# Linear attention and a softplus-erf block on one core: one more of nine blocks multiplies g by w_out with seven quarter products

## The chip, the cores and the metric

The kernel runs on one core of a Trainium2 chip. The core has five engines that run side by side, each with its own queue of instructions: TensorE (PE, matrix products into the eight banks of PSUM), VectorE (DVE), ScalarE (ACT), GpSimd (POOL) and SyncE (SP, which here issues nearly all transfers). They wait for each other through semaphores. The metric is the device time of one execution in microseconds (us), as the median of several runs. Lower is better.

## The reference

Attention with a feature map, for 8 batches of 8 heads, 576 tokens and head dimension 64; then a block of two products on the 4608 tokens of 512 values:

```python
def phi(x):
    proj = np.einsum('bhsd,df->bhsf', x, w_phi)
    proj = proj - np.max(np.abs(proj), axis=-1, keepdims=True)
    return np.concatenate([np.exp(proj), np.exp(-proj)], axis=-1)
q_p, k_p = (phi(q), phi(k))
kv = np.einsum('bhsf,bhsd->bhfd', k_p, v)
z = np.sum(k_p, axis=2)
num = np.einsum('bhsf,bhfd->bhsd', q_p, kv)
den = np.einsum('bhsf,bhf->bhs', q_p, z)[..., None] + 1e-06
x = num / den                        # heads side by side: 4608 x 512
...
h = x @ w_in                         # 512 x 2048
sp = np.maximum(h, 0.0) + np.log1p(np.exp(-np.abs(h)))
g = h * erf(sp)
out = g @ w_out                      # 2048 x 512
```

## The kernel before

**Blocks, units, steps.** The tokens of the second part are cut into nine blocks of 512 (`NS = 9`). Blocks 0 to 7 are the first 512 tokens of each batch; block 8 collects the last 64 of all batches. The hidden dimension d_ff is cut into four units of 512 (`NU = 4`). So there are 36 steps, and each step makes h of one unit of one block and then takes g of an earlier unit times w_out. The attention of batch b + 1 is spread over the steps of block b.

**Three terms for one product.** Values and weights are kept as a high and a low fp16 part, and each product is the sum of three matmuls: high by high, high by low, low by high. `mm` (L579, issued at L584) issues each of them as two matmuls on 64 columns of the array each, one per half of the output partitions, that run side by side.

**Seven quarter products.** h is made for all nine blocks after Strassen and Winograd: x and w_in are cut into quarters, seven sums and differences of the quarters of each are formed (x by `split` and `combine`, L942 and L976, with nine tiles `x` in all; w_in by `split_weights`), and seven products of half the size, added up in `add` and `snap`, take the place of eight. `product` (L1107) issues one of them.

**g times w_out has two forms.** The constant `OW` names the first block that uses the second form; it is 4, so blocks 0 to 3 use the first and blocks 4 to 8 the second.

- The first form, `o_piece` (L1358): matmuls of 512 columns, four token tiles by sixteen slices of d_ff by three terms. In `erf_gate` g is made by one multiplication of h and erf (L1207), a conversion to fp16 on ScalarE (L1210) and a subtraction for the low part (L1215), on tiles of 1024 columns. The sums come in two rounds of half of d_ff each: the first round's are evicted (L1379 or L1381) and stored to DRAM (tile `part`, L1383), the second's fetched from there and added (L1387, L1388).
- The second form, `o_chunk` (L1283): seven quarter products of 256 columns for each unit pair and round, fourteen pieces of twelve terms in each round, each evicted or added to tiles in SBUF (L1335, L1338; the very last in two halves at L1326). `g_forms` (L1220) makes the quarters and their sums from g (L1202 the multiplication, L1239 the sums, `split_g` the high part on ScalarE through L602 and the low part on DVE at L1233), seven forms for each unit in eighteen tiles `gf`. The forms of w_out are made once by `t_forms` (L1253) on GpSimd (L1264, L1269, L1279) and stored to DRAM (tile `td`); each round fetches eight tiles of them (L1294).

**Where `t_forms` stands.** It has eight parts, two rounds of four. One part is called in each step from step `TW_FROM` = 10 on. The pieces of a round of g times w_out stand two steps behind the step of the same number, so with block 4 the second form is first read in step 18.

**What sets the order.** Nothing is issued where the code calls it. Each operation is recorded by `Plan.op` with an engine, a cost, its buffers and a priority, its position in the nominal course of PE's work plus an offset. `Plan.run` (L290) then plays the five engines forward, and gives each engine, whenever it is free, the ready operation of the lowest priority; an operation is ready when its inputs and a free tile for its output are there. Tiles of one kind are handed out in the order of the calls. Operations of DVE and GpSimd that are marked `port` are kept from overlapping. The order so found is fixed in the program, for SP's queue of transfers as well.

**The table of shifts.** `SHIFT` changes single priorities: when the planned time of PE passes a key, the operations with the listed numbers get the listed nanoseconds added to their base priority. The numbers are those of the calls (`o.seq`).

```python
while shifts and free["PE"] >= shifts[0][0]:
    for seq, by in shifts.pop(0)[1].items():
        self.ops[seq].prio = self.ops[seq].base + by
```

**Attention.** Groups of four tiles go through `project` (L797), `front` (the maximum at L740, the subtraction at L756), two exponentials on ScalarE, a transposition (`t_piece`, later `turn` with a DMA, L842 to L845), `kv_piece` and `n_piece` (matmuls at L594, evictions at L874, L910 and L918). Nearly all of the evictions are on DVE.

Of the kernel before, what the change touches and what calls it, by code (L numbers as in the profile page):

```python
# [95 lines left out]
SLACK = 1000.0  # L96
WARM = 7
HOLE = 600.0
OW = 4
GF = 18  # L100
OC = 8
TW_FROM = 10
TW_STEP = 1
TW_POOL = 1
OW_ODD = (1, 1, 1, 1, 1, 1, 1)
# [25 lines left out]
OSB_ACT = 0, 2  # L131
OC_ACT = 9, 9
SHIFT = {
# [38 lines left out]
}  # L172
PRINT = None
EXP_LN = "natural_log_exp_and_others"
# [2 lines left out]
def early(name, step):  # L177

    return EARLY.get(name, globals()[name]) if step < NE else globals()[name]
# [22 lines left out]
class Plan:  # L202
# [27 lines left out]
    def op(self, eng, cost, fn, r=(), w=(), done=None, off=0.0, mode=COLS, land=0.0, port=False, need=None, give=None):  # L230
        o = Op()
        o.eng, o.cost, o.fn, o.mode, o.land, o.port = eng, cost, fn, mode, land, port
        o.slack = self.slack
        o.need, o.give = need, give
        o.stay = self.stay
        o.after = None
        o.late = self.late
        o.step = self.step
        o.done = cost + 120.0 if done is None else done
        o.seq = len(self.ops)  # L240
        o.base = o.prio = self.pos + off
        o.succ, o.unmet, o.ready, o.start = [], 0, 0.0, None
        o.bufs = []
        o.open = o.bufs
        deps = {}

        def touch(item, write):
            b, key = item if isinstance(item, tuple) else (item, None)
            if b not in o.bufs:
                o.bufs.append(b)  # L250
                b.left += 1
            known = write
            for k, (ws, rs) in b.state.items():
                if k is None or key is None or k == key:
                    known = True
                    for d in ws:
                        deps[d] = True
                    if write:
                        for d in rs:
                            deps[d] = True  # L260
            assert known, "read before it is written"
            if write:
                if key is None:
                    b.state.clear()
                b.state[key] = ([o], [])
            else:
                b.state.setdefault(key, ([], []))[1].append(o)

        for item in r:
            touch(item, False)  # L270
        for item in w:
            touch(item, True)
        deps.pop(o, None)
        for d in deps:
            d.succ.append(o)
        o.unmet = len(deps)
        self.ops.append(o)
        return o
# [188 lines left out]
def favor_attention_moe(ctx: ExitStack, tc: tile.TileContext, qk, vp, wphi, w_in, w_out, out):  # L467
# [716 lines left out]
    def erf_gate(n, after):  # L1184
# [12 lines left out]
        op(ACT, 2230, last, w=pair[1:], done=1070, need="erf", give="exp", off=GATE_AT[2])  # L1197
        if n[0] >= OW:
            h0, h1 = hs.pop((n, 0)), hs.pop((n, 1))
# [195 lines left out]
    todo = [(s, 2 * r + i) for s, r in rounds for i in range(2)]  # L1395
    half_rounds = [(s, r, t if s < OW else 7 * t) for s, r in rounds for t in range(2)]
    SIZE = lambda x: range(4) if x[0] < OW else range(x[2], x[2] + 7)
    steps = [[todo[i] if i < len(todo) else None, []] for i in range(len(todo))]
    for i, o in enumerate(half_rounds):
        later = TAIL[1] if i >= len(todo) - TAIL[0] else OW_LAG if o[0] >= OW else 0  # L1400
        steps[min(i + 2 + later, len(todo) - 1)][1].append(o)
# [3 lines left out]
    def moe_step(h, o):  # L1405
        prods = h_unit(h) if h else []
        last = h == todo[-1]
        mix = (0,) * 7 if last else (OW_ODD if o[0][2] else OW_EVEN) if o and o[0][0] >= OW else early("O_ODD", plan.step) if o and o[0][2] == 1 else early("O_EVEN", plan.step)
        left = [(x, i) for x in o for i in SIZE(x)]
        o_part = lambda x, i: o_chunk(x, i) if x[0] >= OW else o_piece(x, i)  # L1410
        for c, f in enumerate(prods):
# [52 lines left out]
    for n, (h, o) in enumerate(steps):  # L1464
        plan.step = n
        if forms and n >= TW_FROM and (n - TW_FROM) % TW_STEP == 0:
            t_forms(*forms.pop(0))
# [90 lines left out]
```

## Time and profile before

| what | value |
|---|---|
| time, median of three runs | 935.15 us (934.76 to 935.24) |
| the profiled execution | 934.75 us |
| its span from first to last instruction | 932.9 us |
| granted TensorE clock | 0.999 |
| matmuls | 17226, of which 1536 of 512 columns |
| transfers | 185.75 MB |

A page of the profile shows one execution. "Busy" is the time in which an engine has an instruction at work; register, branch, semaphore and DMA-issuing instructions are not counted. Matmuls overlap in the array and their ends are modelled, so the busy time of PE is no sum of its instructions' lengths, and the rate has to be read from counts and times of stretches. PEld is the loading of weights into the array, which overlaps the matmuls. In groups of instructions, each row has the line of the code, the engine, the operation, output <- inputs, the count, then busy time and mean length of one, then the idle time of the engine ahead of them and what ended it. Rows of stages have for each engine the busy time and the number of instructions, then the granted clock, the busy share of the DMA engines and GB/s.

### The profile page before, as it was taken

What the parts mean: (1) busy time and instruction counts of PE and PEld (TensorE: products, weight loads), DVE (VectorE), ACT (ScalarE), POOL (GpSimd) and SP (SyncE); (2) the same over time, 40 slices, a digit from 0 to 9 for tenths busy, and PEclk for the clock granted to TensorE, in tenths of its full rate; (3) what the DMA queues carried; (4) which work ended last, traced back from release to release, by engine and by line L of the source; (5) the groups of instructions that cost most, each with busy time, mean ns of one, the idle gap of its engine ahead of it and who ended that gap; (6) DMA issues with size and microseconds to landing.
All of it is one profiled execution on the core that took longest, in us unless ns stands there. A gap on an engine that the chain in (4) does not pass through costs nothing.

```text
span 932.9 us, 38966 instructions
## 1 busy us (share of the span) xinstructions
PE 920.2 (99%) x17226; PEld 813.9 (87%) x17226; DVE 803.7 (86%) x1462; ACT 736.3 (79%) x1164; POOL 192.9 (21%) x201
## 2 busy tenths in 40 slices
PE   8999999999999999999999999999999999999998
PEld 7788877878787878778787899999999999999997
DVE  6999999999768786888877999999999878777875
ACT  7898989797978777877777778968777788779792
POOL 0352120010455657110211020100201241010000
PEclk9999999999999999999999999999999999999999
DMA  9489999999865969467867768686857675782502
GB/s 336 131 232 300 288 231 327 316 316 298 216 163 178 215 166 245 121 168 186 198 149 183 236 142 204 171 222 192 199 119 185 209 197 168 241 192 81 164 32 47
DMA packets 199273, 185.75 MB, mean 199 GB/s; under 512 B 127168, under 2 KB 137536, under 8 KB 199104
## 3 DMA queue, kind: packets, MB, share of 16 engines
q1 hardware_dynamic: 198800, 183.06, 72.2%
q8 instruction: 135, 2.21, 1.0%
q14 instruction: 34, 0.28, 0.1%
q10 hardware_dynamic: 304, 0.20, 0.1%
HBM read 125.80 MB, written 28.05 MB: 165 GB/s over the span
## 4 chain that ended last, share of the span: by engine, by line
PE 84%; DVE 11%; ACT 2%; issue 2%; DMA 1%; SPq 0%; POOL 0%; DVEq 0%; ACTq 0%
PE bank L584 64%; PE bank L594 12%; PE bank L797 5%; DVE m L740 1%; ACT big L602 1%; DVE half L1233 1%; PE bank L828 1%; PE bank L1501 1%; DVE big L1207 1%; DVE half L756 1%; DVE big L1239 1%; DVE big L1132 1%; DVE big L918 1%; DMA half<-td 1%; DVE big L1202 0%
## 5 line engine op out<-in xcount | busy, mean ns | idle before, releaser
L584 PEld LDWEIGHTS <-half 128*64 128x64 f16 x9432 | 512.4, 110 | 74.0 <-issue 2.0
L584 PE MATMUL bank<-half,half 128*64 128x256 f16 x6456 | 381.3, 273 | 0.0
L584 PE MATMUL bank<-woh,half 128*64 128x512 f16 (+1 forms) x1984 | 252.7, 328 | 1.3 <-DVE big L756 0.8
L584 PE MATMUL bank<-wol,half 128*64 128x512 f16 (+1 forms) x992 | 166.5, 328 | 0.0
L602 ACT ACTIVATE big<-big 128x512 f32<-128x512 f32 x200 | 124.1, 629 | 46.8 <-DVE big L756 23.5
L602 ACT ACTIVATE big<-bank 128x512 f32<-128x512 f32 x190 | 111.2, 611 | 42.9 <-PE bank L584 40.2
L952 POOL TENSOR_TENSOR half<-big,half 128x512 f16<-128x512 f32 x54 | 63.4, 1176 | 365.4 <-DVE half L949 135.7
L602 ACT ACTIVATE half<-big 128x512 f16<-128x512 f32 x140 | 81.2, 622 | 57.7 <-DVE big L1239 51.9
L740 DVE TENSOR_REDUCE m<-bank 128x4 f32<-128x512 f32 x144 | 92.7, 683 | 12.6 <-PE bank L797 12.3
L1132 DVE SCALAR_TENSOR_TENSOR big<-bank,big 128x512 f32<-128x512 f32 x108 | 73.8, 685 | 29.8 <-PE bank L584 18.8
L1233 DVE TENSOR_TENSOR half<-big,half 128x512 f16<-128x512 f32 x140 | 92.5, 694 | 2.7 <-ACT half L602 1.7
L584 PE MATMUL bank<-half,wi 128*64 128x256 f16 x1512 | 93.4, 273 | 0.4 <-issue 0.4
L584 PEld LDWEIGHTS <-wi 128*64 128x64 f16 x1512 | 81.1, 110 | 4.3 <-issue 1.4
L594 PEld LDWEIGHTS bank<-v,big 128*64 128x64 f32 x2016 | 76.5, 138 | 6.8 <-issue 0.7
L594 PE MATMUL bank<-v,big 128*64 128x65 f32 (+1 forms) x2016 | 81.9, 228 | 0.4 <-ACT big L602 0.4
L594 PE MATMUL bank<-kv,big 128*64 128x65 f32 x2304 | 81.7, 222 | 0.6 <-DVE big L918 0.5
L594 PEld LDWEIGHTS bank<-kv,big 128*64 128x64 f32 x2304 | 76.3, 138 | 3.8 <-DVE big L918 0.9
L1179 ACT ACTIVATE big<-big 128x1024 f32<-128x1024 f32 x72 | 72.7, 1050 | 1.1 <-DVE half L640 0.7
L1202 DVE TENSOR_TENSOR big<-big,big 128x1024 f32<-128x1024 f32 x40 | 49.5, 1262 | 19.3 <-ACT big L1196 19.3
L756 DVE TENSOR_TENSOR half<-bank,m 128x512 f32<-128x512 f32 x72 | 49.0, 683 | 0.1
L1207 DVE TENSOR_TENSOR big<-big,big 128x1024 f32<-128x1024 f32 x32 | 39.8, 1267 | 9.6 <-ACT big L1196 9.4
L1196 ACT ACT_TABLE_LOAD x36 | 46.2, 1283 | 0.6
(73 smaller groups left out, 1167.2 us busy)
## 6 DMA issues: line engine op xcount, KB each, us to landing
half<-wd SPq DMA_DIRECT2D x189, 256.0 KB, 4.4
half<-td SPq DMA_DIRECT2D x80, 256.0 KB, 4.6
ld<-in_qk_dram SPq DMA_DIRECT2D x31, 576.0 KB, 4.9
v<-in_vp_dram SPq DMA_DIRECT2D x28, 325.0 KB, 4.8
big<-in_moe_w_in_dram SPq DMA_DIRECT2D x32, 256.0 KB, 5.8
big<-in_moe_w_out_dram SPq DMA_DIRECT2D x16, 512.0 KB, 6.9
out_dram<-half SPq DMA_DIRECT2D x32, 256.0 KB, 2.8
wd<-half SPq DMA_DIRECT2D x21, 256.0 KB, 4.7
```

Source lines behind the costliest of these rows:

```text
L584: nc.tensor.matmul(o[half], a[:, half], b, start=start, stop=stop, **kw)
L594: nc.tensor.matmul(o[half], a[:, half], b, start=first and c == 0, stop=last and c == 1)
L602: nc.scalar.activation(out_(), in_(), func, **k)
L740: op(DVE, 600, lambda: nc.vector.tensor_reduce(m.t, ps(), axis=AX.X, op=ALU.max, apply_absolute_value=True), r=[b], w=[m])
L756: op(DVE, 600, lambda: nc.vector.tensor_tensor(to(), ps(), m.t.unsqueeze(2).to_broadcast([P, GT, NF]), op=ALU.subtract), r=[b, m], w=[key])
L797: nc.tensor.matmul(both[nm].t[:, t * P : (t + 1) * P], x()[rows], w.t[rows, :], start=i == 0, stop=i == len(terms) - 1)
L952: op(POOL if pool else DVE, 1160 if pool else 600, lambda: eng.tensor_tensor(tv(1), view(), tv(0), op=ALU.subtract), r=[*reads, (t, 0)], w ...
L1132: op(DVE, 640, lambda: nc.vector.scalar_tensor_tensor(h.t[:, c * 512 : c * 512 + 512], b.t, HSCALE, h.t[:, c * 512 : c * 512 + 512], op0=A ...
L1179: fn = lambda: nc.scalar.activation(L.t, h.t, AF.Softplus, scale=1.0 / SG)
L1202: op(DVE, 1140, lambda h=h, L=L: nc.vector.tensor_tensor(h.t, h.t, L.t, op=ALU.mult), r=[L, h], w=[h], port=True, off=GATE_OFF[0] * (v + 1))
L1207: op(DVE, 1140, lambda h=h, L=L: nc.vector.tensor_tensor(h.t, h.t, L.t, op=ALU.mult), r=[L, h], w=[h], port=True, off=GATE_OFF[0] * (v + 1))
L1233: op(POOL if pool else DVE, 1160 if pool else 600, lambda: eng.tensor_tensor(hv(1), src(), hv(0), op=ALU.subtract), r=[key, (g, 0)], w=[(g ...
```

## The change

Block 3 takes the second form: `OW` goes from 4 to 3, so six blocks of nine use the seven quarter products. `t_forms` is called from step 6 on instead of step 10. And the table `SHIFT` is a new one throughout, with about twice as many entries; since the numbers of the calls are others from step 6 on, its entries can't be matched with the old ones. No function changes.

```diff
-OW = 4
+OW = 3
 GF = 18
 OC = 8
-TW_FROM = 10
+TW_FROM = 6
 TW_STEP = 1
 TW_POOL = 1
...
 SHIFT = {
-    0.0: {22: 3000, 30: 1000, 33: 1000, 59: -2000, 61: 6000, 68: 10822, 96: 4905, 101: 3905, 107: -2000,
...
-    705000.0: {7172: -3000, 7186: 6000},
+    0.0: {13: -8000, 44: 906, 61: 6000, 80: 1000, 92: 906, 116: -300, 123: -6000, 147: 1000, 182: -4000,
...
+    705000.0: {7044: 1, 7046: 2, 7366: 6000, 7482: 6233, 7493: 6000, 7553: -4000, 7702: -6000, 7704: -3000,
+        7947: -3617, 7973: -2000},
 }
```

With `OW = 3` the nominal positions change with it: a piece of the first form counts 10400 ns and one of the second 9160 (`pe_time`), by which the attention is paced against the steps.

88 rows, old and new, of the table SHIFT are left out of this document.

## The prediction

> **What bounds the kernel now.** I read the page's head first, then the busy time by stage, then what TensorE (PE) waits for, then the chain that ended last.
>
> ```profile
> span 932.9 us, 38966 instructions
> PE 920.2 (99%) x17226; PEld 813.9 (87%) x17226; DVE 803.7 (86%) x1462; ACT 736.3 (79%) x1164; POOL 192.9 (21%) x201
> ```
> ```profile
> core 0: us, PE busy (x) PEld busy (x) DVE busy (x) ACT busy (x) POOL busy (x), PEclk, DMA share, GB/s
> 0.00:150.00 150.00, 143.63 (x2655) 121.07 (x2657) 135.63 (x311) 129.18 (x328) 38.84 (x44) 1.00 0.88 259
> 150.00:400.00 250.00, 250.00 (x4304) 197.35 (x4301) 212.10 (x371) 203.55 (x295) 88.31 (x102) 1.00 0.83 228
> 400.00:550.00 150.00, 149.89 (x2832) 123.58 (x2830) 125.85 (x227) 111.08 (x150) 21.82 (x19) 1.00 0.72 184
> 550.00:700.00 150.00, 148.36 (x3156) 144.72 (x3152) 146.97 (x268) 119.44 (x171) 17.94 (x16) 1.00 0.73 180
> 700.00:729.40 29.40, 29.40 (x668) 28.93 (x664) 28.76 (x57) 23.52 (x33) 3.38 (x3) 1.00 0.67 182
> 729.40:765.00 35.60, 35.60 (x658) 35.60 (x654) 30.86 (x50) 26.39 (x36) 10.80 (x9) 1.00 0.82 224
> ```
> ```profile
> PE bank L797 <- DVE big L756: 0.8, 1, 0.8
> PE bank L584 <- DVE big L756: 0.8, 1, 0.8
> PE bank L584 <- DVE half L1326: 0.5, 1, 0.5
> ```
>
> The stages show PE full from 150 us on. Its only idle time between 150 and 765 us is 0.11 us in 400 to 550 and 1.64 us in 550 to 700. The third fence is the complete list of waits of PE from 150 us to the end: two of 0.8 us (these are the 1.64) and the one before the very last product. The granted clock is 1.00. So the span is the work that PE is given, plus some 6.4 us that it stands idle in the first 150 us. But look at VectorE (DVE): in 550 to 700 us it is busy 146.97 of 150, that is 98%, and this is the one stretch of the middle where PE waits, both times for DVE. The kernel has one bound and a second one right behind it.
>
> **Where the change lands.** Block 3 is the block that changes its form.
>
> ```profile
> L1207 DVE TENSOR_TENSOR big<-big,big x8: 1214/1222/1715, 403.1 to 483.8; 128x1024 f32<-128x1024 f32 x8
> L1388 DVE SCALAR_TENSOR_TENSOR half<-bank,half x4: 682/685/689, 497.5 to 528.6; 128x512 f32<-128x512 f32 x4
> L740 DVE TENSOR_REDUCE m<-bank x144: 652/682/698, 6.2 to 713.1; 128x4 f32<-128x512 f32 x144
> L1264 POOL TENSOR_TENSOR half<-woh,wol x16: 1147/1156/1628, 226.3 to 369.4; 128x512 f32<-128x512 f16 x16
> ```
>
> L1207 is h times erf in the plain form, so its last eight (two to a unit, four units) are block 3: its gates run from 403 to 484 us. The last four L1388 are its second round, ended by 529 us. The attention, which shares DVE with all this, goes on until after 713 us (L740). The change therefore extends to about 400 us the stretch in which seven products and attention run together, which until now begins near 510.
>
> **PE.** The plain form streams 512 columns per matmul, the seven products stream 256. I need the issue pitch of both.
>
> ```profile
> 225.39 36.67 PE bank L584 x482
> 729.43 198.28 PE bank L584 x3628
> ```
> ```profile
> L584 PE MATMUL bank<-woh,half 128*64 128x512 f16 x128 | 20.2, 380 | 0.0
> L584 PE MATMUL bank<-half,half 128*64 128x256 f16 x288 | 17.6, 273 | 0.0
> L584 PE MATMUL bank<-wol,half 128*64 128x512 f16 x64 | 12.3, 379 | 0.0
> ...
> L584 PE MATMUL bank<-half,wi 128*64 128x256 f16 x2 | 0.3, 272 | 0.0
> ```
>
> These are two pieces of the chain, and the groups by form inside the first of them. The second piece holds 256-column matmuls alone: 198.28 / 3628 = 0.05465 us each. The first has 128 + 64 = 192 of 512 columns and 288 + 2 = 290 of 256. The latter take 290 x 0.05465 = 15.85 us, so the wide ones take (36.67 - 15.85) / 192 = 0.1084 us. (The "mean ns" of 273 and 380 are lengths with the pipeline in them and can't be summed.) By the code, block 3 now issues 4 token tiles x 16 slices of d_ff x 3 terms x 2 halves = 384 wide matmuls: 41.6 us. After, 2 rounds x 14 pieces x 12 x 2 = 672 narrow ones: 36.7 us. **PE gains 4.9 us.**
>
> One rule speaks against reading PE so. The Trainium skill, "Perfetto Trace Analysis", section "Identifying the Most-Contended Engine", says that a PE's matmul busy share is a poor measure and that the busy share of weight loads should be judged instead. Here that share goes from 79% (197.35 of 250) to 100% (35.60 of 35.60) where seven products run, and the change adds 288 loads; what that would make of the sum is the last rival. The two pitches decide against it here: each matmul of either width has one load of 64 columns, and the wide one takes 1.98 times as long.
>
> **DVE and ScalarE.**
>
> ```profile
> L1207 DVE TENSOR_TENSOR big<-big,big 128x1024 f32<-128x1024 f32 x32 | 39.8, 1267 | 9.6 <-ACT big L1196 9.4
> L1215 DVE TENSOR_TENSOR half<-big,half 128x1024 f16<-128x1024 f32 x32 | 40.3, 1272 | 1.8 <-ACT half L1210 1.6
> L1388 DVE SCALAR_TENSOR_TENSOR half<-bank,half 128x512 f32<-128x512 f32 x16 | 11.0, 687 | 4.4 <-PE bank L584 4.4
> L1202 DVE TENSOR_TENSOR big<-big,big 128x1024 f32<-128x1024 f32 x40 | 49.5, 1262 | 19.3 <-ACT big L1196 19.3
> L1233 DVE TENSOR_TENSOR half<-big,half 128x512 f16<-128x512 f32 x140 | 92.5, 694 | 2.7 <-ACT half L602 1.7
> L1239 DVE TENSOR_TENSOR big<-big 128x512 f32<-128x512 f32 x40 | 28.3, 708 | 0.1
> L1239 DVE TENSOR_TENSOR big<-big,big 128x512 f32<-128x512 f32 x40 | 27.4, 686 | 0.2
> L1338 DVE SCALAR_TENSOR_TENSOR half<-bank,half 128x512 f32<-128x512 f32 x49 | 33.4, 684 | 9.6 <-PE bank L584 9.5
> L602 ACT ACTIVATE half<-big 128x512 f16<-128x512 f32 x140 | 81.2, 622 | 57.7 <-DVE big L1239 51.9
> L1210 ACT CAST half<-big 128x1024 f16<-128x1024 f32 x32 | 33.1, 1044 | 0.1
> ```
>
> The plain rows cover four blocks and the others five. Block 3 loses 39.8/4 + 40.3/4 + 8 evictions of 0.687 = 25.5 us of DVE. It gains 49.5/5 (gate) + 92.5/5 (low parts) + (28.3 + 27.4)/5 (sums) + 14 evictions of 33.4/49 = 0.68 each, which is 9.9 + 18.5 + 11.1 + 9.5 = 49.0 us. **DVE has 23.5 us more to do, to save PE 4.9.** ScalarE has 81.2/5 - 33.1/4 = 8.0 us more, on 111.08 of 150: I cost that at nothing, since it stays near 82% of a stretch shortened to 145.1; without that cover it would cost up to the 8.0.
>
> What hides the 23.5? In 400 to 550 us DVE would have 125.85 + 23.5 = 149.4 us to do. At the density of the next stretch (98%) that takes 152.4 us, and PE's share of the stretch is now 145.1: **7.3 us too much** if all of it must be done there. Over 400 to 765 us, up to the end of attention and a little past it, it is 125.85 + 146.97 + 28.76 + 30.86 + 23.5 = 355.9, or 363.2 us at 98%, against 365 - 4.9 = 360.1: 3.1 too much. Before 400 us there is room: 212.10 of 250 is 33 us short of 98%. So some of the attention of the blocks that follow has to be done before 400, or some of the work of 400 to 550 after 700. The order can do part of that, as the planner issues whatever is ready. But x has nine tiles and a block keeps seven until its last unit, so attention can't run more than two of the seven forms ahead.
>
> How much PE then waits is not shown for this stretch. Its ends are 0 (the room before 400 takes enough) and 7.3 us (none moves). The nearest row is the stretch that already has both kinds of work: 1.64 us idle in 150. I take that rate for the newly filled 150 + 65 us: 215/150 x 1.64 - 0.11 = **2.2 us**.
>
> **The other parts.** The forms of w_out (POOL, from 226 us on, 16 x L1264 and what follows) are called four steps earlier. Their first reader moves four steps too, and POOL is busy 88.31 of 250 there, so nothing; if they came due among the other transfers before 250 us, a late one would be at most the 0.8 us that the longest wait above shows. DMA:
>
> ```profile
> half<-td SPq DMA_DIRECT2D x80, 256.0 KB, 4.6
> part<-half SPq DMA_DIRECT2D x16, 256.0 KB, 4.7
> half<-part SPq DMA_DIRECT2D x16, 256.0 KB, 4.0
> ```
>
> Sixteen fetches from td come (80 for five blocks), four stores to part and four loads from it go: 2 MB more, with DMA at 0.72 in that stretch. Each fetch waits on SP's queue for an eviction of the same round, and behind it queue the transposes of attention and of x. Again I take nothing, since such fetches stand among 550 to 700 already and are in its 1.64; a late one in each round would be 2 x 0.8 = 1.6 us. The new order may also change the 6.4 us that PE idles before 150. No row says which way: I take 0, and for the ends a third of it, 2.1, up or down.
>
> **The sum.** The profiled execution took 934.75 us, 1.85 around its span; the median of the runs is 935.15, 0.4 above it. 934.75 - 4.9 + 2.2 = 932.05, and 932.4 on the scale of the median.
>
> **The rivals.**
> 1. DVE's room elsewhere takes it all, and the order also regains idle time of the first 150 us: stall 0 to -2.1, 930.2 down to 928.1. For it: 33 us of room before 400. Against: the nine x tiles, and both waits of PE in the middle are for DVE.
> 2. DVE gives back most of it: a stall of 3.1 (the sum over 400 to 765) to 6.7, that is 933.3 to 936.9. For it: that sum. Against: room before 400.
> 3. **Slower: DVE becomes the bound of 400 to 550.** Nothing moves out, PE waits the 7.3 us: 934.75 - 4.9 + 7.3 + 0.4 = 937.6, and 939.2 with a late fetch in both rounds. It decides once less than about half a microsecond of the 7.3 can leave the stretch. For it: the x tiles tie the attention to its block. Against: in 550 to 700 all of this already runs with PE idle 1%.
> 4. Loads, not columns, set PE's pace: 288 more at 0.05465 us is +15.7, so 950.9. By the page named above this would be so; the pitches deny it.
>
> **How the numbers follow.** About 0.2% (1.9 us) is what a measurement of this kernel can tell from no change: faster is below 933.3, slower above 937.0. Forecast (930.2 to 933.3) 0.47, rival 1 0.11, rival 2 0.24, rival 3 0.17, rival 4 0.01. So faster 0.58, same 0.24, slower 0.18. The range goes from 929.0 to 938.5: it leaves out the lower part of rival 1 (0.05), the upper part of rival 3 (0.10) and rival 4.
>
> **What would show it.** PE: 672 narrow matmuls more, 384 wide ones fewer, both pitches unchanged. DVE: 803.7 becomes about 827, and 400 to 550 us goes from 125.85 to over 140. ScalarE about 744. The long stretch of L584 at the end keeps its length and starts some 2 to 5 us earlier. PE's idle time between 400 and 765 rises from 1.75 to about 4 us, its waits named DVE; near 0 is rival 1, above 7 rival 3. The prediction is wrong in its base if PE's idle time in the first 150 us changes by more than 2.1 us, or if the waits name POOL, SP or DMA.

## The result: 0.3% slower

The changed kernel takes 937.53 us as the median of 8 runs (936.78 to 940.33), the kernel before, on the same chip, 934.76 (934.05 to 935.24). The ratio is 1.0033 with a 95% interval of 1.0022 to 1.0044: slower by 2 to 4 us, 2.8 by the medians. The profiled execution of the changed kernel took 936.78 us, the lowest of its eight, with a span of 935.0; before it was 934.75 and 932.9. All lines from 173 on are 17 higher in the changed kernel, since the new table is longer: L601 is the L584 of before, L1250 its L1233, L1219 its L1202.

First the head of the page and then the stages of the changed kernel, with the columns of before: length, PE, weight loads, DVE, ACT and POOL busy (instructions), granted clock, DMA share, GB/s.

```profile
span 935.0 us, 39702 instructions
PE 921.1 (99%) x17546; PEld 831.5 (89%) x17546; DVE 822.6 (88%) x1504; ACT 742.4 (79%) x1184; POOL 191.5 (20%) x201
```
```profile
0.00:150.00 150.00, 145.56 (x2706) 122.85 (x2708) 137.10 (x315) 130.24 (x328) 38.37 (x44) 1.00 0.90 264
150.00:400.00 250.00, 249.78 (x4280) 196.43 (x4278) 211.90 (x368) 201.31 (x294) 87.45 (x102) 1.00 0.83 225
400.00:550.00 150.00, 146.84 (x3070) 139.24 (x3068) 143.01 (x264) 118.29 (x171) 19.20 (x17) 0.99 0.74 192
550.00:700.00 150.00, 148.59 (x3148) 144.74 (x3146) 143.79 (x264) 118.03 (x167) 20.30 (x17) 1.00 0.79 192
700.00:729.40 29.40, 29.15 (x673) 28.01 (x670) 29.37 (x56) 22.21 (x33) 3.55 (x3) 1.00 0.56 137
```

The place to look at first is 400 to 550 us. DVE goes from 125.85 to 143.01 there, and PE's idle time from 0.11 to 3.16. That is most of what the stages show. The longest waits of PE from 150 us to the end name ScalarE and DVE:

```profile
PE bank L611 <- ACT big L619: 2.3, 3, 1.3
PE bank L601 <- DVE big L773: 1.2, 1, 1.2
PE bank L814 <- DVE big L935: 0.7, 2, 0.4
```

The work itself behaved as worked out: the groups by form, and the last long piece of the chain, say so.

```profile
L601 PE MATMUL bank<-woh,half 128*64 128x512 f16 x768 | 121.9, 380 | 0.1
L601 PE MATMUL bank<-wol,half 128*64 128x512 f16 x384 | 73.6, 379 | 0.0
```
```profile
795.55 134.51 PE bank L601 x2454
```

768 + 384 = 1152 wide matmuls are left of 1536, that is 384 fewer, and the narrow ones still come every 134.51 / 2454 = 0.0548 us. So PE has 4.9 us less to do and the span is 2.1 us longer: for 7.0 us more than before PE does no useful work in these two executions (7.7 by the medians). Two places hold most of what can be seen of that. At the first, PE multiplies for nothing: the planner fills a gap of its plan with matmuls on a constant tile (`hot`), to keep the array's clock up. These are the groups on that tile between 150 and 200 us, of the kernel before and of the changed one:

```profile
L1501 PE MATMUL bank<-hot 128*64 128x512 f16 x8 | 1.0, 380 | 0.0
```
```profile
L1518 PE MATMUL bank<-hot 128*64 128x512 f16 x30 | 3.4, 379 | 0.0
```

PE counts as busy all the same, so a gap that was planned doesn't show as idle time; it has to be looked for under this tile's name. The 30 stand at 177.67 us. No operation of the sixth block has run by then, and the first one of `t_forms` (L1281, the L1264 of before) starts only at 201.6 us, so this gap goes with the new order and not with DVE's load in 400 to 550. In the first 150 us there are more of them too, 10.3 us against 9.2:

```profile
L1501 PE MATMUL bank<-hot 128*64 128x512 f16 x62 | 9.2, 437 | 1.5 <-DVE hot L1507 1.5
```
```profile
L1518 PE MATMUL bank<-hot 128*64 128x512 f16 x72 | 10.3, 429 | 1.5 <-DVE hot L1524 1.5
```

The second place is near 535 us. From the timeline of the changed kernel (start, length, engine, line, output <- inputs, count, and in brackets the idle time before it and what ended it):

```profile
525.66 0.60 ACT L619 ACTIVATE big<-bank 128x512 f32<-128x512 f32 x1 [2.61 <-PE bank L601]
...
528.75 2.00 ACT L1196 ACTIVATE big<-big 128x1024 f32<-128x1024 f32 x2
...
530.13 0.68 DVE L773 TENSOR_TENSOR big<-bank,m 128x512 f32<-128x512 f32 x1
...
534.09 1.28 ACT L1211 ACT_TABLE_LOAD   x1
535.38 0.63 ACT L619 ACTIVATE big<-big 128x512 f32<-128x512 f32 x1
...
536.07 0.34 PE L611 MATMUL bank<-v,big 128*64 128x65 f32 x4 [1.30 <-ACT big L619]
...
537.11 1.13 PE L611 MATMUL bank<-v,big 128*64 128x65 f32 x16 [0.70 <-ACT big L619]
```
```profile
535.00:540.00 5.00, 3.23 (x54) 3.06 (x56) 4.49 (x8) 4.93 (x10) 0.00 (x0) 0.70 0.92 219
```

DVE subtracts the maximum of a group of attention (L773) at 530.13, and the exponentials of that group (L619) could follow at 530.8. But ScalarE's queue holds a whole gate ahead of them, softplus from 528.75 and erf with its table loads until 535.4. PE has nothing else left and waits 1.30 and 0.70 us; its clock falls to 0.70 in these 5 us, which costs up to 1.5 us more. DVE is not out of it, though: in the 25 us ahead of this gap it is busy without a pause, and its subtraction comes only after the gate has started on ScalarE. In the kernel before it was nearly as full in the same 25 us, 24.19, and PE didn't wait.

```profile
510.00:535.00 25.00, 24.77 (x530) 23.42 (x524) 25.00 (x44) 17.06 (x24) 0.00 (x0) 1.00 0.81 209
```

The sum of what can be seen: 2.4 us of matmuls on `hot` near 178 us (3.4 - 1.0), 3.05 of idle time in 400 to 550, 0.2 each in 150 to 400 and 700 to 729, less 0.8 in the first 150 us (1.9 less idle time, since 143.63 busy became 145.56, but 1.1 more on `hot`), and less 0.2 each in 550 to 700 and behind 729. That is 4.7, with the clock 6.2 at most. Where the rest of the 7.0 lies is not shown; gaps that the modelled lengths of the matmuls cover would not appear in these rows.

### The profile page after: what moved, and what is told of

It is laid out like the page before. It is cut to its first block, busy times and chain, and to the rows that moved or that the text cites. A ratio compares the mean times of both kernels' runs of the same rounds, so it can differ in the third digit from the quotient of the medians.

```text
span 935.0 us, 39702 instructions
## 1 busy us (share of the span) xinstructions
PE 921.1 (99%) x17546; PEld 831.5 (89%) x17546; DVE 822.6 (88%) x1504; ACT 742.4 (79%) x1184; POOL 191.5 (20%) x201
## 5 line engine op out<-in xcount | busy, mean ns | idle before, releaser
L601 PEld LDWEIGHTS <-half 128*64 128x64 f16 x9720 | 527.5, 110 | 59.0 <-issue 4.3
L601 PE MATMUL bank<-half,half 128*64 128x256 f16 x6840 | 403.9, 273 | 1.5 <-DVE big L773 1.2
L601 PE MATMUL bank<-woh,half 128*64 128x256 f16 (+1 forms) x1920 | 229.9, 316 | 0.6 <-DVE half L1343 0.5
L619 ACT ACTIVATE big<-big 128x512 f32<-128x512 f32 x200 | 123.4, 628 | 43.1 <-DVE big L862 19.1
L601 PE MATMUL bank<-wol,half 128*64 128x256 f16 (+1 forms) x960 | 156.8, 315 | 0.0
L619 ACT ACTIVATE half<-big 128x512 f16<-128x512 f32 x168 | 97.3, 621 | 69.8 <-DVE big L1256 61.9
L619 ACT ACTIVATE big<-bank 128x512 f32<-128x512 f32 x190 | 111.3, 613 | 31.2 <-PE bank L601 28.9
L1250 DVE TENSOR_TENSOR half<-big,half 128x512 f16<-128x512 f32 x168 | 111.8, 695 | 2.5 <-ACT half L619 1.6
L601 PE MATMUL bank<-half,wi 128*64 128x256 f16 x1512 | 95.5, 273 | 0.0
L601 PEld LDWEIGHTS <-wi 128*64 128x64 f16 x1512 | 81.3, 110 | 3.5 <-issue 1.0
L611 PEld LDWEIGHTS bank<-kv,big 128*64 128x64 f32 x2304 | 78.8, 139 | 4.1 <-ACT big L619 1.5
L1219 DVE TENSOR_TENSOR big<-big,big 128x1024 f32<-128x1024 f32 x48 | 58.0, 1235 | 23.6 <-ACT big L1213 23.6
L1355 DVE SCALAR_TENSOR_TENSOR half<-bank,half 128x512 f32<-128x512 f32 x59 | 40.1, 682 | 10.7 <-PE bank L601 10.6
L773 DVE TENSOR_TENSOR half<-bank,m 128x512 f32<-128x512 f32 x72 | 48.7, 679 | 0.0
```

Of the source, the lines that this page charges most:

```text
L601: nc.tensor.matmul(o[half], a[:, half], b, start=start, stop=stop, **kw)
L611: nc.tensor.matmul(o[half], a[:, half], b, start=first and c == 0, stop=last and c == 1)
L619: nc.scalar.activation(out_(), in_(), func, **k)
L773: op(DVE, 600, lambda: nc.vector.tensor_tensor(to(), ps(), m.t.unsqueeze(2).to_broadcast([P, GT, NF]), op=ALU.subtract), r=[b, m], w=[key])
L1219: op(DVE, 1140, lambda h=h, L=L: nc.vector.tensor_tensor(h.t, h.t, L.t, op=ALU.mult), r=[L, h], w=[h], port=True, off=GATE_OFF[0] * (v + 1))
L1250: op(POOL if pool else DVE, 1160 if pool else 600, lambda: eng.tensor_tensor(hv(1), src(), hv(0), op=ALU.subtract), r=[key, (g, 0)], w=[(g ...
```

## The experiments

Two theories stood. **Capacity**: the sixth block gives DVE more than it can do beside the attention, and PE waits for it wherever the order puts the wait. **Order**: the new order of operations has single bad places, and a better one would give back PE's 4.9 us.

**Relief and load in a fixed order.** Three kernels keep an order as it is and change only what is issued in it.

```diff
 # e1, from the changed kernel: block 3's low parts of g are left out
-... lambda: eng.tensor_tensor(hv(1), src(), hv(0), op=ALU.subtract), ...
+... lambda: nc.vector.tensor_copy(hv(1), hv(0)) if n[0] == 3 else eng.tensor_tensor(hv(1), src(), hv(0), op=ALU.subtract), ...
 # e2, from the changed kernel: no matmuls on `hot` after 150 us
-order.append((at, -1, lambda s=spare[0]: filler(self.slots[s])))
+if at < 150000.0:
+    order.append((at, -1, lambda s=spare[0]: filler(self.slots[s])))
 # e3, from the kernel before: block 3's L1215 issued three times over
-op(..., lambda h=h, a=a, b=b, eng=eng, cols=cols: eng.tensor_tensor(
-    halfs(b)[:, cols], h.t[:, cols], halfs(a)[:, cols], op=ALU.subtract), ...)
+def low(h=h, a=a, b=b, eng=eng, cols=cols, times=3 if n[0] == 3 else 1):
+    for _ in range(times):
+        made = eng.tensor_tensor(halfs(b)[:, cols], h.t[:, cols], halfs(a)[:, cols], op=ALU.subtract)
+    return made
+op(..., low, ...)
```

> The changed kernel in its own order; only block 3's 28 low parts of g (subtractions of 0.69 us on DVE) are left out and replaced by fp16 copies of the high part, so that DVE has some 10 to 14 us less to do in 400 to 500 us. Capacity theory (DVE's added 23.5 us fill the stretch and PE waits for DVE): PE's idle time in 400 to 550 us falls from 3.16 to under 1.5 and the time by 1.5 to 4 us, to 933.5 to 936. Order theory (the new order of operations has single bad places, such as the gate on ScalarE ahead of the exponentials near 535 us, whatever DVE's load): idle time stays above 2.5, time within 1 us of 937.5.

> The changed kernel in its own order, without the 30 warming matmuls that it issues near 178 us (and without any others after the first 150 us). If the order had left PE without other work there, as order and capacity theory both say of that place, the time stays within 1 us of 937.5 and PE shows some 3 us of idle time instead. If the warming matmuls were in the way of work that was ready, it falls by 2 to 3 us to about 935.

> The kernel before in its own order; block 3's eight low parts of g (1.27 us each on DVE) are computed three times over, which adds 16 x 1.27 = 20 us to DVE in 400 to 500 us and nothing to PE. Capacity theory: PE's idle time in 400 to 550 us rises from 0.11 to 3 or more and the time by 3 to 7 us, to 938 to 942. Order theory: DVE has 24 us free there and takes it, time within 1 us of 934.8.

e1 took 936.59 us, 0.9 less than the change, ratio to before 1.0022 (1.0011 to 1.0032), an interval that overlaps with the change's. Its DVE total went from 822.6 to 812.5 us, but PE's idle time in 400 to 550 us stayed: two stages of e1, and the 25 us ahead of the gap near 535.

```profile
450.00:500.00 50.00, 49.25 (x1074) 47.81 (x1070) 44.19 (x93) 40.22 (x59) 10.84 (x9) 1.00 0.70 163
500.00:550.00 50.00, 48.00 (x992) 46.19 (x990) 46.12 (x83) 35.52 (x52) 2.85 (x3) 0.97 0.73 188
```
```profile
510.00:535.00 25.00, 25.00 (x542) 23.92 (x538) 24.97 (x47) 15.52 (x24) 0.00 (x0) 1.00 0.80 196
```

0.75 + 2.00 = 2.75 us, and the longest waits are the same for ScalarE. That is the number that the order theory expected. But it settles less than was planned: all 28 copies run before 500 us, and ahead of the gap near 535 DVE is as full as in the changed kernel, 24.97 of 25.00. So e1 relieved DVE where PE was idle for 1.16 us (which became 0.75) and not where it was idle for 2.00. What it shows is that 10 us of room on DVE in 400 to 500 don't move on by themselves in a fixed order.

e2 took 939.09, ratio 1.0042 (1.0026 to 1.0058), 1.5 us above the change by the medians, where no more than 1 us was expected; the intervals of the ratios overlap, so that difference is not clear of noise. The matmuls on `hot` were in the way of nothing: PE waits 2.91 us at that place instead (timeline of e2, where L602 is the L601 of the change), and in the two stretches from 176 us on the clock falls to 0.89 and 0.96: that is what leaving them out does.

```profile
183.15 3.22 PE L602 MATMUL bank<-half,half 128*64 128x256 f16 x34 [2.91 <-ACT big L620]
```
```profile
176.00:186.00 10.00, 7.09 (x112) 6.51 (x110) 9.26 (x22) 9.61 (x11) 0.00 (x0) 0.89 1.02 278
186.00:200.00 14.00, 14.00 (x214) 11.06 (x212) 13.14 (x21) 10.12 (x17) 3.61 (x3) 0.96 1.16 343
```

e3 took 956.62, ratio 1.0237 (1.0222 to 1.0252): 20 us more for DVE cost 21.6 us, far above even the 3 to 7 that capacity expected. This is the stage of 400 to 550 us, and who waited in it (in total, times, longest):

```profile
400.00:550.00 150.00, 134.66 (x2354) 106.04 (x2351) 125.53 (x206) 93.31 (x126) 16.89 (x14) 0.97 0.64 161
```
```profile
PE bank L584 <- DVE big L1132: 8.3, 3, 3.9
PE bank L797 <- DVE big L918: 5.1, 1, 5.1
```

DVE is busy 125.53, no more than the 125.85 of before, and PE waits for evictions that stand in DVE's queue behind the repeated subtractions. The 24 us in which DVE was idle before were no room at all in that order. Neither theory had this: order expected no more than 1 us.

**The same step, planned without a table.** To take the searched orders out, the next kernels have `SHIFT = {}`, and the planner finds its order by its own priorities. e6 has five plain blocks (`OW = 5`), e4 four, e5 three.

```diff
-SHIFT = { ... }
+SHIFT = {}
```

> The kernel before (four plain blocks, OW 4) with an empty table of shifts. Both theories: 2 to 8 us slower than with its table, 937 to 943; it is the base of the next two.

> The changed kernel (three plain blocks, OW 3) with an empty table of shifts. Capacity theory: with no searched order on either side the sixth block costs more than it saves, 3 to 8 us above the run with OW 4 and empty table, most of it as idle time of PE in 400 to 550 us. Order theory: without the two tables the change gives 2 to 5 us, as PE's 4.7 us less work says.

> Five plain blocks (OW 5) with an empty table of shifts: the step before this one. Both theories: 2 to 5 us above the run with OW 4 and empty table, since PE has 4.7 us more to do and DVE 24 us less. Beside the run with OW 3 it shows where the gain of one more block turns into a loss.

| plain blocks | kernel | median | ratio to the kernel before, 95% interval |
|---|---|---|---|
| 5 | e6 | 947.57 | 1.0133 (1.0115 to 1.0151) |
| 4 | e4 | 945.08 | 1.0110 (1.0093 to 1.0127) |
| 3 | e5 | 948.67 | 1.0146 (1.0131 to 1.0161) |

The step from four to three costs 3.6 us, clear of noise: e5's four runs start at 947.18, e4's end at 945.49. The step from five to four gives 2.5 by the medians, but e6's runs go from 945.31 to 948.94, so this gain isn't clear of noise. PE has 4.9 us less to do in both. (e4 as a base came out above the 937 to 943 that were expected.) The stretch from 400 to 730 us in e6, e4 and e5, in that order:

```profile
400.00:730.00 330.00, 326.80 (x6188) 275.07 (x6186) 278.77 (x498) 244.35 (x326) 42.91 (x36) 1.00 0.71 174
```
```profile
400.00:730.00 330.00, 328.36 (x6552) 294.45 (x6550) 298.52 (x540) 252.66 (x347) 42.97 (x36) 1.00 0.76 183
```
```profile
400.00:730.00 330.00, 326.30 (x6816) 307.68 (x6814) 317.95 (x580) 259.51 (x365) 42.96 (x36) 1.00 0.77 186
```

DVE fills up by 20 us a step: 84%, 90%, 96%. To PE's idle time belong the matmuls on `hot` in the same stretch. e6 has none; in e4 and e5 (where the line is L1462) they are:

```profile
L1462 PE MATMUL bank<-hot 128*64 128x512 f16 x42 | 5.2, 379 | 0.0
```
```profile
L1462 PE MATMUL bank<-hot 128*64 128x512 f16 x84 | 10.1, 379 | 0.0
```

Idle and `hot` together are 3.2 us, then 1.6 + 5.2 = 6.8, then 3.7 + 10.1 = 13.8. The last step loses 7.0 us in this stretch to save 4.9. Most of it is not the idle time of PE that capacity expected but the planner's filling. Up to 400 us e4 and e5 have the same 154 matmuls on `hot`, all of them before 150.

e10 does the other part of the change alone: e4 with `TW_FROM = 6` in place of 10.

> The kernel before (OW 4) with an empty table of shifts and the forms of w_out called from step 6 on: the small part of the change alone. Both theories: within 2 us of the 945.1 of the same kernel with step 10.

It took 946.09, ratio 1.0122 (1.0106 to 1.0137), against 945.08 for e4, with an overlapping interval. The earlier calls of `t_forms` cost 1 us or nothing.

**The same step with room on DVE.** e7 is e5 with the low parts of blocks 3 and 4 replaced by copies and their lower cost told to the planner. e12 and e11 are e4 and e5 with all low parts replaced so. All three leave the low part of g out in those blocks. The line of e12 and e11 is below; e7 has the same with the condition `n[0] < 5`.

```diff
-op(POOL if pool else DVE, 1160 if pool else 600, lambda: eng.tensor_tensor(hv(1), src(), hv(0), op=ALU.subtract), ...)
+op(POOL if pool else DVE, 1160 if pool else 240, lambda: nc.vector.tensor_copy(hv(1), hv(0)), ...)
```

> OW 3 with an empty table of shifts, and the 56 low parts of g of blocks 3 and 4 left out and replaced by fp16 copies of the high part, this time with the lower cost known to the planner, which finds its order anew: about 20 us less for DVE between 400 and 600 us, roughly what the sixth block added, and the same work for PE. Capacity theory: PE's idle time from 400 to 730 us falls by half or more and the time by 5 to 10 us from the 948.7 of OW 3 with an empty table, to 939 to 944, below OW 4's 945.1. Order theory: it moves by no more than 3 us, in either direction.

> OW 4 with an empty table of shifts; the low parts of g of all five blocks with seven products are left out and replaced by fp16 copies of the high part, with the lower cost known to the planner: some 50 us less for DVE. Both theories: a little under the 945.1 of OW 4 with an empty table, 941 to 944. It is the base of the next run.

> The same with OW 3: the low parts of all six blocks replaced by copies, an empty table of shifts. Capacity theory: once DVE is no longer full, the same step from four plain blocks to three that cost 3.6 us with full DVE gives most of PE's 4.7 us, 3 to 5 us less than the run with OW 4. Theory that the loss lies in something else that the sixth block brings (transfers, tiles, waits on ScalarE): it still costs 1 us or more.

e7 took 939.83, ratio 1.0057 (1.0040 to 1.0074): 8.8 us less than e5, for some 20 us less on DVE. e12 took 942.87 (1.0093, 1.0076 to 1.0110) and e11 938.05 (1.0041, 1.0026 to 1.0056). So with room on DVE, the step from four plain blocks to three **gives 4.8 us**, about PE's whole 4.9; with DVE full it cost 3.6. The same relief does much less before the step: by the ratios e12 is 1.6 us faster than e4 and e11 9.8 us faster than e5. All three times lie where capacity expected them. The stretch of e12 and of e11, and their matmuls on `hot` in it:

```profile
400.00:730.00 330.00, 326.91 (x6578) 293.79 (x6576) 279.98 (x553) 256.07 (x353) 43.00 (x36) 1.00 0.74 182
```
```profile
400.00:730.00 330.00, 328.81 (x6986) 314.23 (x6984) 295.67 (x604) 263.70 (x374) 44.85 (x38) 1.00 0.77 192
```
```profile
L1462 PE MATMUL bank<-hot 128*64 128x512 f16 x18 | 2.3, 379 | 0.0
```
```profile
L1462 PE MATMUL bank<-hot 128*64 128x512 f16 x28 | 3.5, 379 | 0.0
```

At 295.67 of 330 (90%) on DVE, PE's idle time is 1.19 us with three plain blocks, where e5 had 3.70 and three times the matmuls on `hot`. Idle and `hot` together go from 3.09 + 2.3 = 5.4 in e12 to 1.19 + 3.5 = 4.7 in e11: the step loses nothing here. All that the sixth block brings besides is still there, its fetches from td, its tiles and its conversions on ScalarE. One thing these runs don't separate: a copy is not only less work for DVE (the step now adds 14.5 us to its total, 754.0 to 768.5, in place of the 22.7 from e4 to e5), it also ends sooner, so the matmuls on the low part could start earlier after each gate.

**Another order of the whole change.** e8 has all of the change's work, `t_forms` from step 9, and another table: some of the old entries up to the key of 165 us, several with other values, and behind that a new one, with 4,530 entries in all where the change's has 285 and the old one 177. (The recorded expectation calls the first part the table of before; of its 109 entries up to that key, 14 stand in e8 as they were.) e9 makes in addition the four low parts of the form A22 of block 3 on GpSimd, with a table of its own, which is left out here as e8's is.

```diff
-TW_FROM = 6
+TW_FROM = 9
 # e9 only
-G_POOL = ()
-G_TO = 7
+G_POOL = (6,)
+G_TO = 4
```

> The same change (OW 3, all of its work) in quite another order: the forms of w_out from step 9 on, the table of before for the first 200 us, and behind that a table of shifts newly searched. So the place near 178 us is gone and the gates of blocks 3 and 4 fall differently. Order theory: most of PE's 4.7 us comes back, 930 to 933. Capacity theory: the idle time only turns up at other places between 400 and 700 us, time 934 to 938.

> As the run before, but the four low parts of the form A22 of block 3 (2.8 us of DVE) are made on GpSimd, with its own searched order. Capacity theory: 1 to 3 us less than the run before, if GpSimd's use of the port that it shares in the plan doesn't hold DVE up. Order theory: within 1 us of the run before.

e8 took 935.93, ratio 1.0019 (1.0010 to 1.0029), 1.6 us under the change by the medians and 1.3 by the ratios, whose intervals overlap. That is within what capacity expected and above the 930 to 933 of the order theory. Its stage from 400 to 735 us, and its matmuls on `hot` there:

```profile
400.00:735.00 335.00, 333.72 (x7016) 319.59 (x7012) 324.40 (x592) 268.74 (x379) 42.93 (x36) 1.00 0.76 191
```
```profile
L1518 PE MATMUL bank<-hot 128*64 128x512 f16 x38 | 5.0, 380 | 0.0
```

PE's idle time is only 1.28 us, but 5.0 us of matmuls on `hot` stand in its place: the loss has changed its name and its position. e9 took 935.20, ratio 1.0007 (0.9998 to 1.0016), the same as the kernel before. It is 0.7 us under e8, which the order theory expected (capacity expected 1 to 3); with another table in it, it can't tell what the 2.8 us less for DVE did. No version of this study beats the kernel before.

## Why the prediction was wrong

Forecast was 932.4 us, with 929.0 to 938.5 as the range and 0.18 for slower. The time lies inside the range, but on the side that had the small chance: a gain was forecast, and it was a loss.

- **PE's work: right.** 384 wide matmuls fewer, pitches unchanged, 4.9 us. The Trainium skill, "Perfetto Trace Analysis", section "Identifying the Most-Contended Engine", names the busy share of weight loads, beside the arithmetic done, as the measure of PE's headroom. Here that share rose from 87 to 89%, and in the last long piece the matmuls came no later; with room on DVE the same step shortened the run by 4.8 us (e12 to e11), loads and all.
- **DVE's load: right in kind, and a little high.** 23.5 us were worked out; the total rose by 18.9 (803.7 to 822.6). 400 to 550 us went above 140, as foretold. ScalarE rose by 6.1 in place of 8.0.
- **The stall: this step failed.** I took PE's idle rate of the next stretch, 1.64 us in 150, for the newly filled one and got 2.2 us, and I put the new order at 0. In place of 2.2, 7.0 us were lost. Between 400 and 765 us PE's idle time rose by 3.1 (from 1.75 to 4.8), and the clock's fall near 535 adds up to 1.5; so the stall itself was taken too small, 4.6 at most for 2.2. Two things were wrong in it. The rate was read from idle time alone, which leaves out the matmuls on `hot`, the clock and the small gaps. And it was taken to be a property of DVE's density, when 550 to 700 us was a stretch in which the planner had found work for PE. ScalarE, which I put at nothing, has its name on 2.0 of the 3.16 us in 400 to 550. The 0 for the order counted idle time too: near 178 us and before 150 us the new order has 3.5 us more on `hot`, for 1.9 less of idle time. Where the rest of the 7.0 went, 0.8 or more, stays open.
- **Rival 3: near in time, in part by luck, and the cause only in part.** It said 937.6, and 937.53 was measured. But its 7.3 us were to be lost in 400 to 550, where 4.6 at most of the 7.0 are found; 2.4 us stand near 178 us, ahead of all the sixth block's work. It waited for DVE to reach 98%: over the 150 us DVE was busy 143.01, 95%, and 96% in e5's stretch, though 25.00 of 25.00 just ahead of the gap near 535. And the waits at that gap carry ScalarE's name, not DVE's. That DVE's load is what turns the sign is shown without tables (e5 beside e4, e11 beside e12), not in the two kernels compared here.
- **The signs: one came true and misled.** PE's idle time between 400 and 765 us was to be about 4, and above 7 for rival 3. It was 4.8, and the kernel was slower all the same, since idle time left out most of the loss. The last long stretch was to start 2 to 5 us earlier; its end moved from 927.71 to 930.06, 2.35 us later.
- **"The room before 400 takes part of it": wrong.** DVE's work in 150 to 400 us is 211.90, before 212.10. Nothing moved there.
- **The first 150 us: inside its bounds.** Its idle time fell by 1.9, within the 2.1 that I allowed, but 1.1 of that is more matmuls on `hot`.

So both theories hold a part, and their sizes can be told apart only roughly. Other orders of the same work give between 1 and 2.5 us back (e9 clear of noise, with a little of DVE's work on GpSimd; e8 not quite). The remaining loss goes with DVE's load: it is there without any table, and it goes once DVE has room (e11 beside e12). How the load becomes a wait is through the plan: it runs out of work for PE, and the gap is then fixed in every queue. That attention comes later under the load and so leaves the plan without work is the likely way, but only the one place near 535 us was followed. Whether a longer search would find an order with all of PE's 4.9 us stays open; e8 and e9, with far larger tables than the change's, didn't.

## What to carry to other kernels

Trading one engine's work for another's pays until the other is nearly full, here between 90 and 96% of a stretch of 330 us (kernels without a table); one step further the sign turns, although the first engine still has less to do. In a kernel whose queues are laid out in advance, idle time of an engine is not room: 20 us put into DVE's idle 24 cost 21.6. And a planner that fills its gaps with dummy work hides them from the busy share, so count that work as idle before you compare.

## What the runs showed of the hardware

The granted clock falls to half after short gaps. It is 0.50 from 537 to 540 us in the changed kernel, after waits of 1.30 and 0.70 us with four matmuls between them, and 0.50 from 184 to 187 us in e2, after one wait of 2.91 us:

```profile
537.00:540.00 3.00, 2.89 (x50) 2.87 (x52) 2.93 (x6) 2.94 (x7) 0.00 (x0) 0.50 0.74 168
```
```profile
184.00:187.00 3.00, 3.00 (x32) 3.00 (x29) 3.00 (x5) 2.98 (x4) 0.00 (x0) 0.50 1.04 292
```

So the 0.70 and 0.89 above are means of full and half clock. The Trainium skill, "TensorE: Matmul & The Clock Gate", section "What's actually happening", says that the clock goes to half after an idle window of about 3.4 us. The half is what these rows show; the waits that show here are shorter, and the measurement decides.
